# A projection by Strassen's seven products, interleaved with the first product, in a fused Mamba-2 and MoE kernel

## The chip, the cores and the metric

The kernel runs on one core of a Trainium2 chip. The metric is device time in microseconds (us) of one execution. Executions of one kernel mostly agree within 0.5% (four runs before: 420.35 to 421.12 us).

## The reference, cut to what matters

A chunked Mamba-2 scan over 4 batches, 8 heads and 768 steps gives 3072 tokens of 256 features, which go through a feed-forward block in fp32:

```python
def _moe_ref(x, w_in, w_out):          # x 3072x256, w_in 256x2048, w_out 2048x256
    h = x @ w_in
    g = h * (1.0 / (1.0 + np.exp(-1.702 * h)))
    return (g @ w_out).astype(np.float32)
```

`x @ w_in` is called the hidden product below, `g @ w_out` the projection. Both have the same number of multiplications.

## The kernel before

Tokens go in six groups of 512 (`NG` = 6). For a group the kernel does 16 hidden blocks of 128 features (`NF` = 16), each with a SiLU on ScalarE, then the projection. The scan of the next group (turn, gain, scores, finish) is placed among the hidden blocks. The kernel uses PSUM as eight banks of 128x512 fp32. Four go round as single banks (`bank`, tag "ff"). The other four are one area (`area`, tag "cb", one buffer), which holds the scores.

```python
    def bank(name):
        return ps.tile([P, 4 * P], FP32, tag="ff", name=name)          # pool: bufs=4

    def area(name):
        return ps.tile([P, R, 4 * P], FP32, tag="cb", name=name, bufs=1)
    ...
    def hidden(g, gT, f):
        h = bank(f"h{g}_{f}")
        for k in range(NK):
            nc.tensor.matmul(out=h, lhsT=w_in[:, k, f * P:(f + 1) * P], rhs=yT[g][:, k],
                             start=(k == 0), stop=(k == NK - 1))
        nc.scalar.activation(gT, h, AF.Silu, scale=GELU_SCALE)
    ...
    def project(g, gT, k):                     # 128 tokens; four of these in a group
        o = bank(f"o{g}_{k}")[:, :DM]
        for f in range(NF):
            nc.tensor.matmul(out=o, lhsT=gT[f][:, k * P:(k + 1) * P], rhs=w_out[:, f],
                             start=(f == 0), stop=(f == NF - 1))
        store(g, k, o)                         # VectorE scales it, SP stores 128 KB
```

Group 0 uses another order of the same matmuls (`project_all`), as the weights are still being unpacked from fp64; the change keeps that.

The kernel fixes the program's order on each engine (its `in_order`): what is emitted behind another instruction of the same engine stands behind it in that engine's queue and, in the timelines below, does not start before it.

## Time and profile before

| | before |
|---|---|
| time, median of 4 runs of the first comparison | 420.69 us (420.35 to 421.12) |
| span of the profiled execution | 418.8 us |
| TensorE busy | 401.9 us, 96% |
| VectorE busy | 163.6 us, 39% |
| group 3, hidden stage and projection | 63.1 us |
| end of the last projection to the end of the span | 3.2 us |

A busy share is an average over the span. The row of tenths tells where in the span it falls; from 90 us on TensorE is full. PEclk is the TensorE clock that was granted, in tenths of full speed; a "5" is half the clock, and an engine at half the clock still counts as busy. So the two rows have to be read together. The prediction shows these lines.

### The profile page before, as it was taken

The numbers are of one execution on the slowest core, as the hardware profiler recorded it, in microseconds if no ns is written. First come the engines' busy times: TensorE is split into PE (matmuls) and PEld (weight loads), VectorE is DVE, ScalarE is ACT, GpSimd is POOL, SyncE is SP. The second block draws the span as 40 slices with busy tenths as digits, with TensorE's granted clock in tenths as the row PEclk, the third lists the DMA queues.
The fourth block names the chain that finished last, engine by engine and source line by source line (L and its number), as shares of the span: only waits on it lengthen the run. The fifth ranks groups of instructions, "written<-read, shape, count | busy, mean of one in ns | idle before, by whom it ended". The sixth has DMA issues, their size and how long they took to land.

```text
span 418.8 us, 5032 instructions
## 1 busy us (share of the span) xinstructions
PE 401.9 (96%) x2046; PEld 257.9 (62%) x2046; DVE 163.6 (39%) x233; ACT 111.4 (27%) x212; POOL 8.9 (2%) x28
## 2 busy tenths in 40 slices
PE   6889995989999999999999999999999999999997
PEld 2354444768544688544688644588644588644885
DVE  3899889683682225324125323025423000000000
ACT  4119964350233200223200223200233300133000
POOL 4100000010000000000000000000000000000000
PEclk9559997999999999999999999999999999999999
DMA  8888929700492000591000590000000000000000
GB/s 188 162 184 199 351 94 131 222 0 2 87 202 101 2 13 25 73 232 49 1 14 25 70 211 35 0 13 27 13 2 0 2 13 25 14 0 0 13 14 26
DMA packets 86263, 29.66 MB, mean 71 GB/s; under 512 B 75936, under 2 KB 79200, under 8 KB 86240
## 3 DMA queue, kind: packets, MB, share of 16 engines
q1 hardware_dynamic: 84160, 29.07, 29.2%
q10 hardware_dynamic: 2080, 0.26, 0.4%
q8 instruction: 16, 0.26, 0.3%
q14 instruction: 7, 0.06, 0.0%
HBM read 26.08 MB, written 3.24 MB: 70 GB/s over the span
## 4 chain that ended last, share of the span: by engine, by line
PE 86%; DVE 5%; ACT 2%; DMA 2%; issue 2%; SPq 1%; POOL 0%; ACTq 0%; DVEq 0%; POOLq 0%
PE h L492 38%; PE o L506 33%; PE o L517 5%; PE area L402 3%; PE area L478 2%; DMA af<-in_a_dram 2%; PE area L470 1%; DVE L L267 1%; SPq L105 1%; PE area L428 1%; PE ab L284 1%; DMA az<-in_a_dram 1%; ACT CT L376 1%; PE cb L402 1%; DVE CsT L386 1%
## 5 line engine op out<-in xcount | busy, mean ns | idle before, releaser
L492 PE MATMUL h<-yT,w_in 128*128 128x512 f32 x384 | 173.9, 599 | 0.4 <-ACT yT L484 0.4
L506 PE MATMUL o<-w_out,gT 128*128 128x256 f32 x640 | 138.9, 379 | 0.0
L506 PEld LDWEIGHTS o<-w_out,gT 128*128 128x128 f32 x640 | 121.6, 190 | 18.7 <-issue 2.4
L492 PEld LDWEIGHTS h<-yT,w_in 128*128 128x128 f32 x384 | 70.2, 190 | 79.8 <-issue 76.7
L495 ACT ACTIVATE gT<-h 128x512 f32<-128x512 f32 x96 | 57.0, 595 | 223.4 <-PE h L492 223.4
L499 DVE TENSOR_SCALAR ob<-o 128x256 f32<-128x256 f32 x24 | 10.1, 424 | 170.6 <-PE o L506 161.9
L267 DVE TENSOR_TENSOR_SCAN L<-a,idents 128x1024 f32<-128x1024 f32 x18 | 41.1, 2281 | 0.0
L517 PE MATMUL o<-w_out,gT 128*128 128x256 f32 x128 | 32.3, 410 | 0.0
L412 DVE TENSOR_TENSOR L<-L,area 128x2048 f32<-128x2048 f32 x10 | 22.9, 2286 | 19.4 <-PE area L402 19.4
L517 PEld LDWEIGHTS o<-w_out,gT 128*128 128x128 f32 x128 | 25.7, 206 | 5.0 <-issue 1.2
L386 DVE TENSOR_TENSOR CsT<-area,since 128x256 f32<-128x256 f32 (+1 forms) x10 | 3.8, 383 | 42.6 <-ACT CT L376 42.6
L146 ACT ACTIVATE z<-e,edge 128x512 f32<-128x512 uint32 x16 | 11.4, 712 | 12.8 <-DVE e L142 12.8
L307 DVE TENSOR_TENSOR_SCAN L<-ab,idents 128x512 f32<-128x512 f32 x12 | 13.7, 1205 | 1.9 <-PE ab L284 1.9
L284 PE MATMUL ab<-X,ones 32*128 32x512 f32 x24 | 9.9, 804 | 2.6 <-DVE S L442 1.6
L147 ACT ACTIVATE p<-z,edge 128x512 uint32<-128x512 f32 x16 | 11.6, 723 | 0.5
L402 PEld LDWEIGHTS area<-CT,BT 32*128 32x128 f32 x160 | 7.2, 184 | 6.9 <-issue 6.4
L402 PE MATMUL area<-CT,BT 32*128 32x256 f32 x160 | 11.5, 400 | 0.0
L141 ACT ACTIVATE m<-bits 128x512 f32<-128x512 uint32 x16 | 10.7, 670 | 1.6 <-DVE w_out L170 1.6
L162 DVE SCALAR_TENSOR_TENSOR m<-u,m 128x512 f32<-128x512 f32 x16 | 11.0, 685 | 0.0
L164 DVE SCALAR_TENSOR_TENSOR p<-bits,p 128x512 uint32<-128x512 uint32 x16 | 11.0, 685 | 0.0
L478 PE MATMUL area<-L,x 128*32 128x128 f32 x320 | 10.8, 276 | 0.0
L484 ACT ACTIVATE yT<-area 128x256 f32<-128x256 f32 x20 | 6.6, 381 | 15.8 <-PE area L478 15.8
(68 smaller groups left out, 160.4 us busy)
## 6 DMA issues: line engine op xcount, KB each, us to landing
a<-scratch SPq DMA_DIRECT2D x18, 512.0 KB, 7.1
bits<-in_moe_w_in_dram SPq DMA_DIRECT2D x8, 512.0 KB, 5.2
bits<-in_moe_w_out_dram SPq DMA_DIRECT2D x8, 512.0 KB, 4.5
out_dram<-ob SPq DMA_DIRECT2D x24, 128.0 KB, 1.7
x<-in_x_dram SPq DMA_DIRECT2D x22, 128.0 KB, 2.9
b<-in_B_dram SPq DMA_DIRECT2D x24, 64.0 KB, 3.3
c<-in_C_dram SPq DMA_DIRECT2D x24, 64.0 KB, 2.7
af<-in_a_dram SPq DMA_DIRECT2D x4, 384.0 KB
```

What stands on the lines that cost most here:

```text
L146: nc.scalar.activation(z, e, AF.Relu, scale=-8.0, bias=edge[:, 0:1])
L147: nc.scalar.activation(p2, z, AF.Relu, scale=-1.0, bias=edge[:, 1:2])
L267: nc.vector.tensor_tensor_scan(out=Ls[p][:, k].rearrange("p r q i -> p (r q i)"), data0=ra.pop(n), data1=idents.rearrange("p h i -> p (h i ...
L284: nc.tensor.matmul(out=ab, lhsT=ones[rows], rhs=fans[p][rows].rearrange("p k q i -> p (k q i)"), start=True, stop=True, tile_position=(32 ...
L307: nc.vector.tensor_tensor_scan(out=flat[p][:, r], data0=ab, data1=idents.rearrange("p h i -> p (h i)")[:, :2 * Q * P], initial=0.0, op0=AL ...
L402: nc.tensor.matmul(out=cb[:, r, k], lhsT=BT[rows, k], rhs=CT[rows, k].rearrange("p q i -> p (q i)"), start=True, stop=True, tile_position= ...
L412: nc.vector.tensor_tensor(out=Lv, in0=Lv, in1=cb.rearrange("p r k e -> p k r e"), op=ALU.mult)
L478: nc.tensor.matmul(out=y[t][D * q:D * q + D, k], lhsT=rx[p][:, k, h], rhs=L[:, k, h // Q, h % Q], start=False, stop=True, tile_position=(0 ...
L492: nc.tensor.matmul(out=h, lhsT=w_in[:, k, f * P:(f + 1) * P], rhs=yT[g][:, k], start=(k == 0), stop=(k == NK - 1))
L495: nc.scalar.activation(gT, h, AF.Silu, scale=GELU_SCALE)
L506: nc.tensor.matmul(out=o, lhsT=gT[f][:, k * P:(k + 1) * P], rhs=w_out[:, f], start=(f == 0), stop=(f == NF - 1))
L517: nc.tensor.matmul(out=o[k // 2][:, k % 2], lhsT=gT[f][:, k * P:(k + 1) * P], rhs=w_out[:, f], start=(f == 0 and k % 2 == 0), stop=(f == N ...
```

## The change

The intent: each pair of feature blocks is treated as a 2x2 block product (two feature blocks, two halves of the outputs, two halves of the tokens). Strassen's scheme in Winograd's form needs seven block products where the direct way needs eight. The sums of weight blocks are made once (`mix_w`), those of activations per group (`mix_g`), all on VectorE. Seven accumulators of half a bank each lie in the four-bank area. The products of a group are interleaved with its hidden blocks (steps H and P). At the end of a group `combine` makes the four result blocks from the seven, and `give` transposes them back, as they come out with features on the partitions. The core of the diff:

```diff
+    def product(g, j):
+        if j == 0:
+            acc[g] = area(f"acc{g}").rearrange("p r (t e) -> p r t e", t=2)
+        B = gT.pop((g, j)).rearrange("p i (t e) -> p i t e", t=2)
+        T = mixed_g.pop((g, j))
+        A, S = w_out[:, 2 * j:2 * j + 2], mixed_w[j]
+        for r, t, lhsT, rhs in (
+                (0, 0, A[:, 0, :P], B[:, 0, 0]),
+                (0, 1, A[:, 1, :P], B[:, 1, 0]),
+                (1, 0, S[:, 1], T[:, 2]),
     ... four more of the seven
+            nc.tensor.matmul(out=acc[g][:, r, t], lhsT=lhsT, rhs=rhs, ...)
+
+    def combine(g):
+        a = acc.pop(g).rearrange("p r t e -> p (r t) e")
     ... tiles u and c
+        nc.scalar.activation(u[:, 0:4:3], a[:, 0:4:3], AF.Copy)
+        for o, v, w in ((u[:, 2], a[:, 2], u[:, 0]),
+                        (u[:, 1:3], a[:, 3:5], u[:, 2:3].to_broadcast([P, 2, HT])),
+                        (c[:, 0], a[:, 1:6:4], u[:, 0:2]),
+                        (c[:, 1, 1], u[:, 2], u[:, 3]),
+                        (c[:, 1, 0], a[:, 6], u[:, 2])):
+            nc.vector.tensor_tensor(out=o, in0=v, in1=w, op=ALU.add)
     ...
+            at(places, "H0", lambda g=g: combine(g - 1))
+            at(places, "H1", lambda g=g: mix_g(g, 0), lambda g=g: give(g - 1))
+            if g + 1 < NG:
+                at(places, "H0", lambda n=n: score(n), lambda n=n: weigh(n))
+                at(places, "H1", lambda n=n: score(n + 1), lambda n=n: weigh(n + 1))
     ...
+        for step in steps:                     # H0 H1 H2 P0 H3 P1 ... P4 H7 P5 P6 P7
+            j = int(step[1:])
+            if step[0] == "H":
+                hidden(g, 2 * j)
+                hidden(g, 2 * j + 1)
+            else:
+                product(g, j)
+            for do in after[g].get(step, []):
+                do()
     ...
+    combine(NG - 1)
+    give(NG - 1)
```

What is listed "at H0" is emitted after the two hidden blocks of step H0, so behind their SiLUs.

More of the change, by code (lines that the diff above doesn't have):

```diff
@@ L178, in spread @@
     def spread(n):
-        ra[n] = wide.tile([P, NH * P], FP32, tag="bits", name=f"a{n}", bufs=AHEAD + 2)
+        if n - 4 in ra:
+            ra[n] = ra[n - 4]
+        else:
+            ra[n] = wide.tile([P, NH * P], FP32, tag="bits", name=f"a{n}", bufs=AHEAD + 2)
         b, c = divmod(n, NC)
@@ L267, in decay @@
         nc.vector.tensor_tensor_scan(
-            out=Ls[p][:, k].rearrange("p r q i -> p (r q i)"), data0=ra.pop(n),
+            out=Ls[p][:, k].rearrange("p r q i -> p (r q i)"), data0=ra[n],
             data1=idents.rearrange("p h i -> p (h i)"), initial=0.0, op0=ALU.mult, op1=ALU.add)
@@ L353, in turn @@
         since_start(p)
+    shared = range(PG, 2 * PG)
     def bank(name):
@@ L362, in turn_only @@
         s = st[p] = {}
-        if p >= PG:
+        if p in shared:
             s["area"] = area(f"area{p}")
-        tp = s["area"][:, 0] if p >= PG else bank(f"tp{p}")
+        tp = s["area"][:, 0] if p in shared else bank(f"tp{p}")
         tp = tp.rearrange("p (j k i) -> p j k i", j=2, k=2)
@@ L396, in score @@
         BT, CT = s.pop("BT"), s.pop("CT")
-        cb = s["area"] if p >= PG else area(f"cb{p}")
+        cb = s["area"] if p in shared else area(f"cb{p}")
         cb = cb.rearrange("p r (k e) -> p r k e", k=2)
@@ L422, in gain @@
         nk = 1 if c + 2 == NC else 2
-        A = st[p]["area"][:, 1] if p >= PG else bank(f"A{p}")
+        A = st[p]["area"][:, 1] if p in shared else bank(f"A{p}")
         A = A[:, :2 * Q * D].rearrange("p (k e) -> p k e", k=2)
@@ L460, in finish @@
             yT[g] = ffn.tile([P, NK, TG], FP32, tag="yT", name=f"yT{g}")
-        y = [s["area"][:, t] if p >= PG else bank(f"y{p}_{t}") for t in range(NK)]
+        y = [s["area"][:, t] if p in shared else bank(f"y{p}_{t}") for t in range(NK)]
         y = [v[:, :2 * P].rearrange("p (k i) -> p k i", k=2) for v in y]
@@ L486, in finish, with hidden @@
                 y[t].rearrange("p k i -> p (k i)"), AF.Copy)
-    def hidden(g, gT, f):
+    gT = {}
+    HT = TG // 2
+    def hidden(g, f):
+        j, i = divmod(f, 2)
+        if i == 0:
+            gT[g, j] = ffn.tile([P, 2, TG], FP32, tag="gT", name=f"gT{g}_{j}", bufs=NF // 2)
         h = bank(f"h{g}_{f}")
@@ L493, in hidden, with store, out_tile, project_all @@
                              start=(k == 0), stop=(k == NK - 1))
-        nc.scalar.activation(gT, h, AF.Silu, scale=GELU_SCALE)
-    def store(g, k, o):
-        ob = ffn.tile([P, DM], FP32, tag="ob", name=f"ob{g}_{k}", bufs=2)
-        nc.vector.tensor_single_scalar(out=ob, in_=o, scalar=1.0 / GELU_SCALE, op=ALU.mult)
-        r0 = g * TG + k * P
-        nc.sync.dma_start(out=out[r0:r0 + P, :], in_=ob)
-    def project(g, gT, k):
-        o = bank(f"o{g}_{k}")[:, :DM]
-        for f in range(NF):
-            nc.tensor.matmul(out=o, lhsT=gT[f][:, k * P:(k + 1) * P], rhs=w_out[:, f],
-                             start=(f == 0), stop=(f == NF - 1))
-        store(g, k, o)
-    def project_all(g, gT, between):
+        nc.scalar.activation(gT[g, j][:, i], h, AF.Silu, scale=GELU_SCALE)
+    def store(g, half, ob):
+        r0 = g * TG + half * HT
+        nc.sync.dma_start(out=out[r0:r0 + HT, :].rearrange("(k p) d -> p k d", p=P), in_=ob)
+    def out_tile(g, half):
+        return ffn.tile([P, 2, DM], FP32, tag="ob", name=f"ob{g}_{half}", bufs=2)
+    def project_all(g, between):
         o = [bank(f"o{g}_{j}").rearrange("p (k e) -> p k e", k=2) for j in range(CG // 2)]
@@ L516, in project_all @@
             for k in range(CG):
-                nc.tensor.matmul(out=o[k // 2][:, k % 2], lhsT=gT[f][:, k * P:(k + 1) * P],
+                nc.tensor.matmul(out=o[k // 2][:, k % 2],
+                                 lhsT=gT[g, f // 2][:, f % 2, k * P:(k + 1) * P],
                                  rhs=w_out[:, f], start=(f == 0 and k % 2 == 0),
                                  stop=(f == NF - 1), skip_group_check=True)
-        for k in range(CG):
-            store(g, k, o[k // 2][:, k % 2])
+        for half in range(2):
+            ob = out_tile(g, half)
+            nc.vector.tensor_single_scalar(out=ob, in_=o[half], scalar=1.0 / GELU_SCALE,
+                                           op=ALU.mult)
+            store(g, half, ob)
@@ new lines, with mix_w @@
+    mixed_w, mixed_g, acc, done = {}, {}, {}, {}
+    def mix_w(n):
+        t = wide.tile([P, 2, 4, P], FP32, tag="bits", name=f"mw{n}", bufs=AHEAD + 2)
+        w = w_out[:, 4 * n:4 * n + 4].rearrange("p (j i) (c e) -> p j i c e", i=2, c=2)
+        a11, a12, a21, a22 = w[:, :, 0, 0], w[:, :, 1, 0], w[:, :, 0, 1], w[:, :, 1, 1]
+        s1, s2, s3, s4 = (t[:, :, i] for i in range(4))
+        for o, u, v, op in ((s1, a21, a22, ALU.add), (s2, s1, a11, ALU.subtract),
+                            (s3, a11, a21, ALU.subtract), (s4, a12, s2, ALU.subtract)):
+            nc.vector.tensor_tensor(out=o, in0=u, in1=v, op=op)
+        for k in range(2):
+            mixed_w[2 * n + k] = t[:, k]
@@ new lines, in mix_g @@
+    def mix_g(g, j):
+        B = gT[g, j].rearrange("p i (t e) -> p i t e", t=2)
+        t = mixed_g[g, j] = ffn.tile([P, 4, HT], FP32, tag="gT", name=f"mg{g}_{j}", bufs=NF // 2)
+        nc.vector.tensor_tensor(out=t[:, 0:2], in0=B[:, :, 1], in1=B[:, 0], op=ALU.subtract)
+        nc.vector.tensor_tensor(out=t[:, 2], in0=B[:, 1, 1], in1=t[:, 0], op=ALU.subtract)
+        nc.vector.tensor_tensor(out=t[:, 3], in0=B[:, 1, 0], in1=t[:, 2], op=ALU.subtract)
+    def product(g, j):
[8 more added lines that the diff above has]
+                (1, 0, S[:, 1], T[:, 2]),
+                (1, 1, S[:, 0], T[:, 0]),
+                (2, 0, S[:, 2], T[:, 1]),
+                (2, 1, S[:, 3], B[:, 1, 1]),
+                (3, 0, A[:, 1, P:], T[:, 3])):
+            nc.tensor.matmul(out=acc[g][:, r, t], lhsT=lhsT, rhs=rhs,
+                             start=(j == 0 and t == 0), stop=(j == NF // 2 - 1),
+                             skip_group_check=True)
@@ new lines, in combine @@
+    def combine(g):
+        a = acc.pop(g).rearrange("p r t e -> p (r t) e")
+        u = ffn.tile([P, 4, HT], FP32, tag="gT", name=f"u{g}", bufs=NF // 2)
+        c = done[g] = ffn.tile([P, 2, 2, HT], FP32, tag="gT", name=f"c{g}", bufs=NF // 2)
+        nc.scalar.activation(u[:, 0:4:3], a[:, 0:4:3], AF.Copy)
[5 more added lines that the diff above has]
+            nc.vector.tensor_tensor(out=o, in0=v, in1=w, op=ALU.add)
@@ new lines, in give @@
+    def give(g):
+        c = done.pop(g)
+        for t in range(2):
+            o = bank(f"oT{g}_{t}").rearrange("p (k e) -> p k e", k=2)
+            for k in range(2):
+                for i in range(2):
+                    nc.tensor.transpose(out=o[:, k, i * P:(i + 1) * P],
+                                        in_=c[:, i, t, k * P:(k + 1) * P], identity=ident)
+            ob = out_tile(g, t)
+            nc.scalar.activation(ob, o, AF.Copy, scale=1.0 / GELU_SCALE)
+            store(g, t, ob)
@@ L592 @@
         at(in_project[0], i, lambda k=k: spread(2 * CG + k))
-    for k, i in enumerate((0, 1, 5, 7)):
-        at(in_hidden[1], i, lambda k=k: decay(2 * CG + k))
-    scan_at(in_hidden[1], 2 * PG, (3, 4, 5, 8))
-    scan_at(in_hidden[1], 2 * PG + 1, (9, 10, 11, 14))
-    for g in range(1, NG - 1):
-        for j in range(PG if g > 1 else 0):
-            scan_at(in_hidden[g], (g + 1) * PG + j, [8 * j + i for i in (0, 1, 2, 6)])
-        if g + 2 < NG:
-            for k in range(CG):
-                at(in_project[g], k, lambda g=g, k=k: decay((g + 2) * CG + k))
@@ L605, with late @@
-    bring = {g: ((g + 2) * CG, (g + 3) * CG) for g in range(NG - 2)}
-    for g in range(NG):
+    after = [{} for _ in range(NG)]
+    for g in range(1, NG):
+        n, places = (g + 1) * PG, after[g]
+        chunks = range((g + 2) * CG, (g + 3) * CG) if g + 2 < NG else ()
+        if g == 1:
+            def late(p):
+                gain(p)
+                keep(p)
+                score(p)
+                weigh(p)
+            at(places, "H0", lambda: decay(2 * CG), lambda: decay(2 * CG + 1), lambda: turn(n1))
+            n1 = n
+            at(places, "H1", lambda: late(n1), lambda: decay(2 * CG + 2),
+               lambda: decay(2 * CG + 3), lambda: turn(n1 + 1))
+            at(places, "H3", lambda: finish(n1), lambda: late(n1 + 1))
+            at(places, "H4", lambda: finish(n1 + 1))
+            for k, i in enumerate(("H4", "P0", "P2", "P4")):
+                at(places, i, lambda k=k: mix_w(k))
+            for j in range(NF // 2):
+                at(places, f"P{j - 1}" if j else "H4", lambda j=j: mix_g(1, j))
+        else:
+            at(places, "H0", lambda g=g: combine(g - 1))
[3 more added lines that the diff above has]
+                at(places, "H1", lambda n=n: score(n + 1), lambda n=n: weigh(n + 1))
+            at(places, "H2", lambda g=g: mix_g(g, 1))
+            for j in range(2, NF // 2):
+                at(places, f"P{j - 2}", lambda g=g, j=j: mix_g(g, j))
+            if g + 1 < NG:
+                at(places, "H2", lambda n=n: finish(n))
+                at(places, "P0", lambda n=n: finish(n + 1))
+        for k, c in enumerate(chunks):
+            at(places, f"P{k + 1}", lambda c=c: decay(c))
+        if g + 2 < NG:
+            for k in range(PG):
+                p = (g + 2) * PG + k
+                at(places, f"P{5 + k}", lambda p=p: turn(p), lambda p=p: gain(p),
+                   lambda p=p: keep(p))
@@ L607 @@
+    for f in range(NF):
+        hidden(0, f)
+        for do in in_hidden[0].get(f, []):
+            do()
+    project_all(0, in_project[0])
+    for g in range(1, NG):
         if g + 2 < NG:
-            for j in range(PG if g else 0):
-                load((g + 2) * PG + j)
+            for k in range(PG):
+                load((g + 2) * PG + k)
             for b in range(NB):
@@ L612 @@
                     spread_rows(b)
-        gT = []
-        for f in range(NF):
-            gT.append(ffn.tile([P, TG], FP32, tag=f"gT{f}", name=f"gT{g}_{f}", bufs=1))
-            hidden(g, gT[f], f)
-            for do in in_hidden[g].get(f, []):
-                do()
-        if 0 < g < NG - 2:
-            for n in range(*bring[g]):
-                spread(n)
-        if g == 0:
-            project_all(g, gT, in_project[g])
-            continue
-        for b in list(raf):
-            clip_rows(b)
-            decay_rows(b)
-        for k in range(CG):
-            project(g, gT, k)
-            for do in in_project[g].get(k, []):
-                do()
+                    at(after[g], "P4", lambda b=b: clip_rows(b), lambda b=b: decay_rows(b))
+        ahead = 5 if g == 1 else 3
+        steps = [f"H{j}" for j in range(ahead)]
+        for j in range(NF // 2):
+            steps += [f"P{j}"] + ([f"H{j + ahead}"] if j + ahead < NF // 2 else [])
+        for step in steps:
[3 more added lines that the diff above has]
+                hidden(g, 2 * j + 1)
+            else:
+                product(g, j)
+            for do in after[g].get(step, []):
+                do()
+            if g + 2 < NG and step in ("H1", "H3"):
+                for k in range(2):
+                    spread((g + 2) * CG + k + (2 if step == "H3" else 0))
+    combine(NG - 1)
+    give(NG - 1)
     in_order(tc)
```

## The prediction

It uses these figures of the kernel before. Behind the wait of 4.36 us, which ends when VectorE is done with the rotated C in the area that the gain products share with it, the trace has half the clock from 68.4 to 75.2 us, 6.8 us. An fp32 tensor_tensor of VectorE takes 423 ns for 256 columns, 692 for 512 and 2286 for 2048 (the rows of L386, L170 and L412).

> **What bounds the kernel now.** I read the page first, then the busy time by stage, then TensorE's timeline. The page's busy shares and slices:
>
> ```profile
> PE 401.9 (96%) x2046; PEld 257.9 (62%) x2046; DVE 163.6 (39%) x233; ACT 111.4 (27%) x212; POOL 8.9 (2%) x28
> PE   6889995989999999999999999999999999999997
> PEclk9559997999999999999999999999999999999999
> ```
>
> TensorE is full from about 90 us to the end; no other engine is half busy. Clock dips (5, 5, then 7) stand only in the first fifth. Busy time by stage, a projection and the hidden stage after it (columns: span, then PE, PEld, DVE, ACT, POOL, clock, DMA share, GB/s):
>
> ```profile
> 206.20:233.80 27.60, 27.60 (x129) 24.30 (x128) 8.74 (x9) 0.60 (x1) 0.00 (x0) 1.00 0.04 15
> 233.80:269.30 35.50, 35.45 (x205) 16.79 (x205) 9.69 (x12) 12.28 (x25) 0.00 (x0) 1.00 0.45 93
> ```
>
> Both are TensorE alone. There are six groups of 512 tokens; a middle one takes 206.22 to 269.35 = 63.1 us. Every microsecond of TensorE work taken out counts, and so does every one in which it stands still. TensorE's timeline gives the prices:
>
> ```profile
> 172.32 0.38 PE L369 MATMUL area<-ident,b 128*128 128x128 f32 x2
> 172.54 0.38 PE L369 MATMUL area<-ident,c 128*128 128x128 f32 x2
> ...
> 206.22 27.79 PE L506 MATMUL o<-w_out,gT 128*128 128x256 f32 x128
> ...
> 360.46 27.63 PE L492 MATMUL h<-yT,w_in 128*128 128x512 f32 x64
> ```
>
> The projection of a group is 16 x 4 = 64 matmuls of 256 columns, recorded as 128 passes: 27.63 us to the next stage, 0.216 us a pass, 0.432 us a matmul. One hidden block (two matmuls of 512, four passes of 0.429) is 1.72 us. Four transposes of 128x128 (one pass each) take 172.32 to 172.76 = 0.44 us, 0.11 us each.
>
> Why idleness can cost twice is shown where this kernel waits longest:
>
> ```profile
> 63.01 1.89 PE L517 MATMUL o<-w_out,gT 128*128 128x256 f32 x8
> 69.26 0.44 PE L428 MATMUL area<-x,Be 128*32 128x64 f32 x8 [4.36 <-DVE CsT L386]
> 69.63 8.20 PE L517 MATMUL o<-w_out,gT 128*128 128x256 f32 x24
> ```
> ```profile
> 66.00:68.00 2.00, 0.00 (x0) 0.00 (x0) 1.97 (x3) 0.31 (x1) 0.00 (x0) 1.00 1.12 119
> 68.00:70.00 2.00, 0.74 (x9) 0.57 (x10) 1.40 (x4) 0.00 (x0) 0.00 (x0) 0.60 1.04 143
> 70.00:72.00 2.00, 2.00 (x6) 1.56 (x6) 1.97 (x6) 1.09 (x2) 0.00 (x0) 0.50 1.01 102
> ```
>
> After 4.36 us of idleness the clock falls to 0.50, and the next 24 passes take 0.34 us each instead of 0.216: 3 us more. The same stage's wait of 1.76 us, before 90.07, leaves the clock at 1.00.
>
> [...]
>
> ```profile
> L386 DVE TENSOR_TENSOR CsT<-area,since 128x256 f32<-128x256 f32 x7 | 3.0, 423 | 30.4 <-ACT CT L376 30.4
> L170 DVE TENSOR_TENSOR w_out<-m,p 128x512 f32<-128x512 f32 x8 | 5.5, 692 | 0.3
> L412 DVE TENSOR_TENSOR L<-L,area 128x2048 f32<-128x2048 f32 x10 | 22.9, 2286 | 19.4 <-PE area L402 19.4
> ```
>
> **The change, part by part.** Groups 1 to 5 change; group 0 keeps its direct projection.
>
> *Removed.* 7 products of 256 columns instead of 8 for each of 8 pairs of blocks: 8 matmuls less a group, 8 x 0.432 = 3.45 us; five groups: -17.3 us, all on TensorE.
>
> *Added on TensorE.* The result comes out transposed: 8 transposes a group, 0.88 us. Four groups: +3.5 us; those of group 5 are in the tail below.
>
> *Added beside it.* VectorE gets sums of activations, three instructions for each pair: 0.69 + 0.42 + 0.42 = 1.53 us, 12.3 us a group; once, sums of weights, 16 x 0.42 = 6.8 us; a group's combination, five instructions. With scans (four of 2.28 us) and weighting (two of 2.29) that is some 33 us of VectorE in 63: it fits. In the interleaved part one product step (14 passes, 3.0 us) plus one hidden step (two blocks, 3.4 us) lasts 6.4 us, and the worst VectorE step (1.53 sums, 2.57 scan and its end, in two groups 2.3 for the decay rows) is run off before the step that needs it, as sums are made two steps ahead. I followed which instruction each wait in the built program names and found no other standstill there. Group 1, with sums one step ahead but five hidden steps first, waits perhaps 0.8 us for VectorE's scans. Buffers of sums and activations come free one step early.
>
> *The new wait.* The accumulators occupy the four-bank area that the scores also need. In the built order of groups 2, 3 and 4, TensorE does the first two hidden blocks and then the scores of the next group, which wait for the last of the combination's reads. The combination starts with a ScalarE copy that stands behind the SiLUs of those two blocks. When such blocks follow a projection in the kernel before (they begin at 360.46):
>
> ```profile
> 362.43 0.60 ACT L495 ACTIVATE gT<-h 128x512 f32<-128x512 f32 x1 [28.75 <-PE h L492]
> ...
> 364.15 0.60 ACT L495 ACTIVATE gT<-h 128x512 f32<-128x512 f32 x1 [1.12 <-PE h L492]
> ```
>
> The second SiLU starts 3.69 us after the blocks begin. The copy (128x512, about 0.6) then ends at 4.8. VectorE's five: 0.42 + 0.69 + 0.69, then two of 0.42 that overlap a little, with hand-overs: 2.6, so 7.4 us. TensorE has issued its blocks by 3.43. It stands 3.9 us, three times: **+11.8 us**. Group 5 has no scores, but its transposes after the second hidden step (6.9) wait until 7.4: +0.4.
>
> *The clock.* TensorE idles 3.8 us, and the 1.1 us of scores after it use 32 rows a matmul. [...] With a chance of a bit under a half for each of three: +3 to +3.5 expected, 0 to 9 possible (odds that I chose, as no trace shows a gap of this length). [...]
>
> *The tail.* Now the last projection is followed by:
>
> ```profile
> 415.75 0.42 DVE L499 TENSOR_SCALAR ob<-o 128x256 f32<-128x256 f32 x1 [6.48 <-PE o L506]
> ```
>
> and one store; from 415.56 to 418.8 it is 3.2 us. After the change, behind the last product: 0.2 to completion, copy 0.6, VectorE 2.6, transposes 0.6, two output copies from 4.05 to 5.1, and the store of 256 KB, 2.6 as now and some 0.4 more. That is 8.2: +5.0 us.
>
> Sum: -17.3 + 3.5 + 0.8 + 11.8 + 0.4 + 5.0 = +4.2, or 424.8 us at full clock; with some 2.3 of that loss (I shade it, as it may not come at all), 427.
>
> **The rivals.** (a) *The TensorE work decides*: if the wait for the area were short, 420.6 - 17.3 + 3.5 + 5 = 412. For it: TensorE is the bound, and 8 of 64 matmuls go. Against: the order of instructions is fixed, the copy cannot pass the SiLUs, and nothing of TensorE's can pass the scores. (b) *The clock falls at every boundary*: 424.8 + 9 = 434. For it: 4.36 us did it in this trace. Against: 1.76 us did not, 3.8 lies between[...]. (c) *VectorE becomes the bound of the interleaved part*: each of 40 steps late by 0.5 us gives 445. Against: 33 of 63 us, and sums two steps ahead.
>
> **Range and chances.** Without clock loss 424.8, give or take 1.5; with it up to 434. Range 422.5 to 433. Faster by over 2% is below 412.2: only rival (a), 0.04. Slower by over 2% is above 429.0: clock lost at two boundaries or more, 0.35. Within 2%: 0.61.
>
> **What would show it.** TensorE's idle time before the scores of groups 2 to 4: 3.8 us each, put down to VectorE's combination; if it is under 1 us, the main step is wrong. The clock in the stretch after them: 1.00 or 0.50. Product passes at 0.216 us and 112 a group; if 0.25 or more, the interleaving costs. Idle time before products after the first: near zero; if VectorE's sums are named there, rival (c). Last product to end: about 8 us. Group period 64.7 us against 63.1. I am wrong if the scores don't wait, or if the clock falls in stretches other than after those waits.

## More of the kernel before

Faster or slower means a difference of over 2%.

## The result, and the profile after

The changed kernel takes 430.58 us (median of 4 runs, 429.2 to 431.3) against 420.69. The ratio is 1.0231, with a 95% interval of 1.0202 to 1.026: slower. Ratios in this document are the mean time of one kernel's fast runs over that of the other's fast runs of the same rounds, so they are not quite the ratio of the medians quoted.

The page's shares and slices of the kernel after:

```profile
PE 395.3 (92%) x2006; PEld 251.5 (59%) x2006; DVE 232.5 (54%) x372; ACT 119.9 (28%) x227; POOL 8.9 (2%) x28
PE   6789995989999999699999699999699999999993
PEclk9559996999999999899999899999889999999997
```

TensorE is busy for 6.6 us less, so work was taken away, although part of that busy time now runs at half the clock. Yet the span grew by 8.7 us. There are three new notches in the row of tenths, each a "6", at equal distances, and a lower clock just behind each. They lie at the starts of groups 2, 3 and 4. TensorE's timeline at the first of them:

```profile
168.43 3.60 PE L508 MATMUL h<-yT,w_in 128*128 128x512 f32 x8
175.86 1.15 PE L412 MATMUL cb<-CT,BT 32*128 32x256 f32 x16 [3.84 <-DVE c L592]
176.94 5.40 PE L508 MATMUL h<-yT,w_in 128*128 128x512 f32 x8
```

The number in brackets is the idle time ahead of a row and what ended it. The scores (L412) stand 3.84 us and are released by VectorE's last sum of the combination (L592). The eight hidden passes behind them take 5.40 us, where eight behind scores at full clock take 3.70. ScalarE and VectorE in the same stretch show what the time goes into:

```profile
170.39 0.60 ACT L511 ACTIVATE gT<-h 128x512 f32<-128x512 f32 x1 [4.17 <-issue]
172.06 0.60 ACT L511 ACTIVATE gT<-h 128x512 f32<-128x512 f32 x1 [1.07 <-PE h L508]
172.55 0.59 ACT L586 ACTIVATE u<-acc 128x512 f32<-128x512 f32 x1
```
```profile
173.18 1.15 DVE L592 TENSOR_TENSOR u<-acc,u 128x256 f32<-128x256 f32 x2 [5.46 <-ACT u L586]
174.36 0.69 DVE L592 TENSOR_TENSOR c<-acc,u 128x512 f32<-128x512 f32 x1
174.97 0.41 DVE L592 TENSOR_TENSOR c<-u 128x256 f32<-128x256 f32 x1
175.30 0.42 DVE L592 TENSOR_TENSOR c<-acc,u 128x256 f32<-128x256 f32 x1
```

The accumulators are complete at about 168.6, but the copy of the combination (L586) starts at 172.55, as two SiLUs stand ahead of it in the queue, and the second of them needs hidden blocks that end at 172. Then VectorE's chain runs to 175.72. In all groups together, from the view of waits (us in total, times, longest):

```profile
PE cb L412 <- DVE c L592: 11.5, 3, 3.8
```

The clock in the first wait and behind it, in stretches of 2 us (the first figure behind the comma is TensorE's busy time, the clock is the figure ahead of the last two):

```profile
172.00:174.00 2.00, 0.02 (x1) 0.00 (x0) 0.79 (x2) 1.08 (x2) 0.00 (x0) 1.00 0.00 0
174.00:176.00 2.00, 0.14 (x4) 0.17 (x8) 1.68 (x4) 0.00 (x0) 0.00 (x0) 1.00 0.00 0
176.00:178.00 2.00, 2.00 (x18) 1.24 (x19) 0.93 (x1) 0.00 (x0) 0.00 (x0) 0.85 0.00 0
178.00:180.00 2.00, 2.00 (x3) 0.67 (x2) 1.97 (x3) 0.00 (x0) 0.00 (x0) 0.50 0.00 0
180.00:182.00 2.00, 2.00 (x5) 0.86 (x4) 0.84 (x2) 0.60 (x1) 0.00 (x0) 0.79 0.00 0
```

The clock stays at 1.00 while TensorE stands, and is then lower by half for (1 - 0.85 + 1 - 0.50 + 1 - 0.79) x 2 / 0.5 = 3.4 us. After the second wait it is 3.4 us again, after the third 6.8 us. Comparing the rows behind each wait (scores, then eight hidden passes) with 1.15 and 3.70 at full clock gives the loss: 5.40 - 3.70 = 1.70; 1.78 + 4.72 - 4.85 = 1.65; 2.09 + 5.70 - 4.85 = 2.94. Together 6.3 us.

The products themselves, from the groups, and the tail, from the timeline of all engines:

```profile
L575 PE MATMUL acc<-mg,mw 128*128 128x256 f32 x240 | 58.3, 379 | 0.0
```
```profile
418.57 0.59 PE L575 MATMUL acc<-mg,w_out 128*128 128x256 f32 x2
419.26 0.60 ACT L586 ACTIVATE u<-acc 128x512 f32<-128x512 f32 x1 [8.53 <-PE acc L575]
...
422.48 1.14 PE L600 MATMUL oT<-ident,c 128*128 128x128 f32 x7 [0.34 <-DVE c L592]
423.07 1.19 ACT L603 ACTIVATE ob<-oT 128x512 f32<-128x512 f32 x2 [3.21 <-PE oT L600]
423.69 0.97 SPq L515 DMA_DIRECT2D out_dram<-ob  x2
```

The products on sums have no idle time ahead of them (the last figure, 0.0). The last pass is issued by 419.0 (418.57 and two of 0.216), and the span ends at 427.5: 8.5 us in place of 3.2.

An account of the two spans: products -17.3 (five groups, 8 matmuls of 0.432 us less), transposes of four groups +3.5, three waits of 4.0 us of lost issue (171.86 to 175.86) +12.0, clock +6.3, tail +5.3, a wait of 0.2 at group 5's transposes. The sum is +10.0, the spans differ by 8.7. The 1.3 us left over were not pursued; turn and gain now follow each other directly, which may save hand-overs, but that is not shown.

### The profile page after: what moved, and what is told of

Read it like the earlier page. It is cut to its first block, busy times and chain, and to the rows that moved or that the text cites. A ratio compares the mean times of both kernels' runs of the same rounds, so it can differ in the third digit from the quotient of the medians.

```text
span 427.5 us, 5052 instructions
## 1 busy us (share of the span) xinstructions
PE 395.3 (92%) x2006; PEld 251.5 (59%) x2006; DVE 232.5 (54%) x372; ACT 119.9 (28%) x227; POOL 8.9 (2%) x28
## 4 chain that ended last, share of the span: by engine, by line
PE 84%; DVE 8%; issue 2%; DMA 2%; ACT 2%; SPq 1%; DVEq 0%; POOL 0%; ACTq 0%; POOLq 0%
PE h L508 39%; PE acc L575 29%; PE o L527 5%; PE cb L412 3%; PE y L488 2%; DVE c L592 2%; PE y L480 1%; DMA af<-in_a_dram 1%; DVE u L592 1%; SPq L110 1%; PE oT L600 1%; DVE L L275 1%; PE tp L379 1%; PE ab L292 1%; ACT u L586 1%
## 5 line engine op out<-in xcount | busy, mean ns | idle before, releaser
L557 DVE TENSOR_TENSOR mg<-gT 128x512 f32<-128x512 f32 x40 | 27.5, 688 | 91.5 <-ACT gT L511 88.4
L575 PE MATMUL acc<-mg,mw 128*128 128x256 f32 x240 | 58.3, 379 | 0.0
L575 PEld LDWEIGHTS acc<-mg,mw 128*128 128x128 f32 x240 | 45.6, 190 | 6.2
L575 PE MATMUL acc<-gT,w_out 128*128 128x256 f32 x160 | 42.1, 386 | 0.0
L575 PEld LDWEIGHTS acc<-gT,w_out 128*128 128x128 f32 x160 | 29.6, 190 | 15.2 <-issue 11.5
L527 PE MATMUL o<-w_out,gT 128*128 128x256 f32 x128 | 32.3, 410 | 0.0
L527 PEld LDWEIGHTS o<-w_out,gT 128*128 128x128 f32 x128 | 25.6, 206 | 5.0 <-issue 1.2
L412 PE MATMUL cb<-CT,BT 32*128 32x256 f32 x160 | 17.0, 495 | 11.5 <-DVE c L592 11.5
L592 DVE TENSOR_TENSOR u<-acc,u 128x256 f32<-128x256 f32 (+1 forms) x10 | 5.6, 558 | 36.3 <-ACT u L586 36.1
L575 PE MATMUL acc<-gT,mw 128*128 128x256 f32 x80 | 23.8, 379 | 0.0
L575 PE MATMUL acc<-mg,w_out 128*128 128x256 f32 x80 | 23.8, 379 | 0.0
L412 PEld LDWEIGHTS cb<-CT,BT 32*128 32x128 f32 x160 | 10.9, 231 | 16.3 <-issue 14.7
L559 DVE TENSOR_TENSOR mg<-gT,mg 128x256 f32<-128x256 f32 x40 | 17.0, 425 | 1.4
L558 DVE TENSOR_TENSOR mg<-gT,mg 128x256 f32<-128x256 f32 x40 | 17.0, 424 | 1.4
```

The lines of the kernel that those rows point to most:

```text
L412: nc.tensor.matmul(out=cb[:, r, k], lhsT=BT[rows, k], rhs=CT[rows, k].rearrange("p q i -> p (q i)"), start=True, stop=True, tile_position= ...
L527: nc.tensor.matmul(out=o[k // 2][:, k % 2], lhsT=gT[g, f // 2][:, f % 2, k * P:(k + 1) * P], rhs=w_out[:, f], start=(f == 0 and k % 2 == 0 ...
L557: nc.vector.tensor_tensor(out=t[:, 0:2], in0=B[:, :, 1], in1=B[:, 0], op=ALU.subtract)
L558: nc.vector.tensor_tensor(out=t[:, 2], in0=B[:, 1, 1], in1=t[:, 0], op=ALU.subtract)
L559: nc.vector.tensor_tensor(out=t[:, 3], in0=B[:, 1, 0], in1=t[:, 2], op=ALU.subtract)
L575: nc.tensor.matmul(out=acc[g][:, r, t], lhsT=lhsT, rhs=rhs, start=(j == 0 and t == 0), stop=(j == NF // 2 - 1), skip_group_check=True)
```

## The experiments

The theory: the time is lost in one wait, of the scores for the accumulators, which is long only because the combination is queued behind two SiLUs, and in the half clock that this idleness brings. Rivals: VectorE's new sums, or the switching between two kinds of matmul, slow the interleaved part; or the clock falls for a reason other than idleness. Each run had three rounds beside the kernel before on the same chip (before: 420.86 in the first four, 420.59 in the last four, single runs 420.16 to 423.2). All results were correct. The argument rests on how the runs differ from the changed kernel and from each other.

### The combination first

```diff
-            at(places, "H0", lambda g=g: combine(g - 1))
...
+        if g > 1:
+            combine(g - 1)
         for step in steps:
```

> Only change: the combination of a group (its ScalarE copy and five VectorE sums) is put ahead of the first two hidden blocks of the next group, not behind their SiLUs. Theory (the scores' wait for the accumulators, and the half clock after it, cost the time): the copy starts 0.2 us after the last product, the sums end 3.3 us later, so the scores are free at 3.5 us against 3.43; three waits of 3.84 us go to under 0.4 us each, the clock stays at 1.00 after group 0, and the time is 412 to 414 us. Rival A (VectorE's sums or the mix of matmuls in the interleaved part cost the time): stays above 425. Rival B (the waits matter but the clock loss has another cause): about 419.

Measured: 411.86 us (410.8 to 414.0), ratio 0.9794 (0.9762 to 0.9825). It does the same work as the changed kernel, with 3 x 6 instructions of the group boundaries moved ahead of two hidden blocks (and 6 at group 5), and takes 18.7 us less. Its timeline at the first boundary, all engines:

```profile
170.43 3.60 PE L508 MATMUL h<-yT,w_in 128*128 128x512 f32 x8
170.69 0.60 ACT L586 ACTIVATE u<-acc 128x512 f32<-128x512 f32 x1 [2.46 <-PE acc L575]
...
173.45 0.42 DVE L592 TENSOR_TENSOR c<-acc,u 128x256 f32<-128x256 f32 x1
...
174.01 1.15 PE L412 MATMUL cb<-CT,BT 32*128 32x256 f32 x16
175.09 3.70 PE L508 MATMUL h<-yT,w_in 128*128 128x512 f32 x8
```

The copy starts 0.26 us after the first hidden pass, not 4.1. The scores have no bracket: TensorE waits for nothing, and the passes behind them take 3.70 us. The expectation was met but for 0.1 us (412 to 414 was expected), and rivals A and B fall: sums and interleaving are all still there, and the clock loss went with the wait (the clock is 1.00 from 170.43 us to 402.7).

### The scores one step later

```diff
-                at(places, "H0", lambda n=n: score(n), lambda n=n: weigh(n))
-                at(places, "H1", lambda n=n: score(n + 1), lambda n=n: weigh(n + 1))
+                at(places, "H1", lambda n=n: score(n), lambda n=n: weigh(n))
+                at(places, "H2", lambda n=n: score(n + 1), lambda n=n: weigh(n + 1))
```

> The combination stays behind the SiLUs; the scores of the next group's two pairs are moved one hidden step later each. Theory: the wait shrinks from 3.84 us to about 0.5 us at the transposes and up to 0.7 us at the first product, the clock stays at 1.00, 415 to 418 us. Rival (it is the combination's own length or its place that costs, whoever comes after it): no change from 430.

Measured: 416.38 us (414.64 to 417.14), ratio 0.9889 (0.9861 to 0.9917). The combination is as late as in the changed kernel, but its consumer comes later. What is left are waits of 0.21 us at the transposes and up to 0.97 at the first product, which needs the area that the second scores now leave later:

```profile
184.99 1.13 PE L575 MATMUL acc<-gT,w_out 128*128 128x256 f32 x4 [0.97 <-DVE L L422]
```

So it is the distance between the combination and its consumer that counts, not where the combination stands.

### Filling the wait, whole and half

```diff
+                at(places, "H0", lambda: fill(4))      # in the second run fill(2)
+    def fill(n):
+        t = bank("fill")
+        for i in range(n):
+            nc.tensor.matmul(out=t, lhsT=ones, rhs=ones.unsqueeze(1).to_broadcast([P, 4, P]),
+                             start=True, stop=True, skip_group_check=True)
```

(The line stands between the combination and the scores, for groups 2 to 4.)

> As the changed kernel, but TensorE does four matmuls of 512 columns on constants (8 passes, 3.43 us) into a spare bank just ahead of the waiting scores; nothing reads them. The wait for the combination is not shortened; TensorE is merely busy in it. Theory: idle time falls under 0.6 us each, the clock stays at 1.00, and the time falls by the clock loss alone (about 6.3 us): 424 to 425. Rival (the half clock comes from something else than the idleness): 430 or more, clock as now.

Measured: 423.78 us (423.51 to 424.03), ratio 1.0071 (1.0056 to 1.0086). Unread matmuls made the kernel 6.8 us faster than the changed one. The waits are 1.2 us in total, and the clock is 1.00 from 160 us to 380. This prices the two halves of the loss apart: 6.8 us for the clock, and from here to the run with the combination first another 11.9 us for the wait.

> The same with two matmuls (4 passes, 1.72 us), which leaves about 2.1 us idle before the scores. [...] no fall, 424 to 425. [...] some or all of the three falls remain, 426 to 431. The wait of 1.76 us in the kernel before did not do it.

Measured: 423.88 us median, but 423.68 to 426.8; ratio 1.0096 (1.0057 to 1.0134). In the profiled run a wait was

```profile
176.66 1.15 PE L419 MATMUL cb<-CT,BT 32*128 32x256 f32 x16 [2.12 <-DVE c L599]
```

and the clock stayed at 1.00 from 160 to 380 us. Of the two outcomes, no fall or some of the three, the profiled run has the first, with a wait of 2.12 us; the changed kernel lost the clock behind waits of 3.84. The one run at 426.8 had a mean clock of 0.949, against 0.958 to 0.962 in the other three. It has no trace of its own, so where it lost the clock is not shown.

### The interleaving without Strassen

```diff
+    def product(g, j):
+        if j == 0:
+            acc[g] = area(f"acc{g}")
+        B = gT.pop((g, j))
+        for i in range(2):
+            for k in range(CG):
+                nc.tensor.matmul(out=acc[g][:, k // 2, (k % 2) * DM:(k % 2 + 1) * DM],
+                                 lhsT=B[:, i, k * P:(k + 1) * P], rhs=w_out[:, 2 * j + i], ...)
     ... combine: two scaled copies by VectorE and two stores, ahead of H0; no sums, no transposes
```

> The interleaving of hidden and product steps and the early combination are kept, but each product step does the eight direct matmuls (no sums, no combination, no transposes; two banks of the area copied out by VectorE, 2 x 0.69 us, before the scores need it). Theory (interleaving is free, Strassen's seven of eight products is what gains): as the kernel before within 1.5 us, 420 to 422 us, so that the seven products with their transposes back are worth 8 to 10 us net against the run with the combination first. Rival (switching between the two kinds of matmul costs): over 424.

Measured: 421.11 us (420.27 to 422.89), ratio 1.0005 (0.9964 to 1.0045). Interleaving alone neither costs nor gains. The seven products are therefore worth 421.11 - 411.86 = 9.3 us net, tail and transposes included. (The two runs came on different chips; by their ratios to the kernel before, 1.0005 - 0.9794, it is 8.9 us.)

### The sums twice

```diff
         nc.vector.tensor_tensor(out=t[:, 0:2], in0=B[:, :, 1], in1=B[:, 0], op=ALU.subtract)
+        nc.vector.tensor_tensor(out=t[:, 0:2], in0=B[:, :, 1], in1=B[:, 0], op=ALU.subtract)
```

(On top of the combination first.)

> As the run with the combination first, but the first of the three sums of each block pair is done twice: VectorE gets 0.69 us more in each of 40 steps, 5.5 us a group. Theory (VectorE has slack behind TensorE): 411.5 to 414, within 2 us of that run. Rival (VectorE is near the bound of the interleaved part): 417 or more, up to 439 if every step is late.

Measured: 412.67 us (412.4 to 413.67), ratio 0.9803 (0.9764 to 0.9843). VectorE works 27 us more (260.2 us busy against 233 in the run without the doubling), and the time moves by 0.8 us. One wait appears, in group 1, where sums are made one step ahead:

```profile
164.06 1.56 PE L576 MATMUL acc<-mg,mw 128*128 128x256 f32 x6 [0.99 <-DVE mg L559]
```

So VectorE is not the bound, and group 1 is the place where it is nearest.

### The last group direct

```diff
-    combine(NG - 1)
-    give(NG - 1)
+    for k in range(CG):
+        g = NG - 1
     ... as project() of the kernel before, from the new tiles
```

(On top of the combination first; group 5 has its hidden blocks first, then this.)

> As the run with the combination first, but group 5, behind which nothing hides the combination and the transposes, keeps the direct projection with its hidden stage ahead of it. It gives back 3.45 us of products and gets the old tail of 3.2 us for one of 9.0. Theory: 411.9 - 9.0 + 3.2 + 3.45 = about 409.5 us. Rival (the tail is set by the store alone): 413 or more.

Measured: 410.25 us (409.54 to 411.11), ratio 0.9742 (0.9709 to 0.9776). The gain is 1.6 us where 2.4 was expected; the two runs came in different rounds, and both of them spread by more than 1.5 us, so the size is uncertain.

### Filling the waits of group 0

```diff
+    at(in_project[0], 1, lambda: fill(5))
+    at(in_project[0], 8, lambda: fill(2))
```

(On top of the last group direct. The kernel before has these waits too.)

> As the run with the last group direct, and TensorE does unread matmuls on constants in the two waits of group 0's projection (4.3 us in the wait of 4.36, 1.7 us in that of 1.76), which the kernel before has too. Theory (idleness alone halves the clock): no half clock after 35 us, 3 us less for the first and 0 to 1.7 for the second, which halved the clock in only some runs: 405 to 407 us, and a smaller spread between runs. Rival: no change from the run with the last group direct.

Measured: 407.41 us (406.66 to 408.18), ratio 0.9674 (0.9641 to 0.9707): the fastest, 13.2 us under the kernel before, and 0.4 us over what the theory allowed. The clock row of its page:

```profile
PEclk9558999999999999999999999999999999999999
```

There is no half clock left after the start. Compared with the run before it this is 2.8 us. The trace of that run has some 3.4 us of half clock behind each of the two waits of group 0 (mean clock 0.91 from 60 to 80 us, 0.94 from 80 to 107), so about 1.7 us were lost at each.

The wait of 1.76 us in group 0 adds something. In the kernel before, and then in the run with the combination first, the same place of the same work reads:

```profile
90.07 0.43 PE L428 MATMUL area<-x,Be 128*32 128x64 f32 x16 [1.76 <-DVE CsT L386]
90.43 3.72 PE L517 MATMUL o<-w_out,gT 128*128 128x256 f32 x16
```
```profile
90.17 0.43 PE L438 MATMUL area<-x,Be 128*32 128x64 f32 x16 [1.76 <-DVE CsT L396]
90.53 5.41 PE L527 MATMUL o<-w_out,gT 128*128 128x256 f32 x16
```

The same idle time costs nothing in one execution and 1.7 us in another. Behind this wait the clock was read in seven traces: it is 0.50 from 92 to 95 us with the combination first and with the direct products interleaved, 0.50 from 91 to 94 with the last group direct, and stays at 1.00 in four (before, after, scores later, sums twice).

## Why the prediction was right or wrong

By its range (422.5 to 433.0) the prediction held at 430.58. The point, 427.0, was 3.6 us low, and the largest single chance, 0.61, was put on within 2%; it came 2.3% slower.

- **The wait**: 3.9 us, three times, named with its cause, from the built order and the durations before. The trace has 4.0 us of lost issue, 3.84 of idleness, and the run with the combination first shows that nothing else made it long. Right.
- **The gain of the products**: the 14 passes of one step took 3.02 us in the trace (154.35 to 157.37), 0.216 each as assumed, with no idle time ahead of them. The run that keeps the direct products confirms the net worth, 9.3 us; the prediction's own terms give 17.3 - 3.5 - 5.0 = 8.8. Right.
- **The clock** is the term that was mis-sized. The prediction counted 2.3 us, shaded down from 3 to 3.5, from "a chance of a bit under a half for each of three", odds that were the author's estimate, as no trace then had a gap of this length. Measured: 6.3 us in the trace, 6.8 by filling the wait; the clock fell at all three.

  What stood ahead of the falls: the changed kernel's trace has them at 177.42, 242.27 and 307.12 us, 64.85 us from one to the next. All falls in the clock records of this trace and of that of the kernel before lie whole multiples of 3.41 us apart, and the half clock lasted 3.41, 3.41 and 6.83 us. So stretches of 3.41 us are compared here. In the one ahead of the second fall TensorE idled for 3.0 us, ahead of the third for 3.1. The one ahead of the first (174.0 to 177.4) holds 1.86 us of idleness, 1.1 us of scores of 32 rows and 0.5 us of hidden passes. The one before that (170.6 to 174.0) holds 1.98 us of idleness and 1.4 us of hidden passes, and the clock was still 1.00 from 174.0 to 177.4. So the idle time of such a stretch did not by itself tell whether the clock fell. What decides is not shown by these runs, nor what odds would have been right. The mean clocks point to falls in the runs without a trace too: (1 - mean clock) x span / 0.5 gives 45 to 52 us of half clock in each of the four runs of the changed kernel, 32 to 35 in those with the whole wait filled. With 6.3 in place of 2.3 the sum would have been 431, partly by luck, as the 0.8 us of the next point did not come.
- **Group 1's wait for VectorE**, 0.8 us: none; the trace shows that stage full. **Group 5's transposes**, 0.4: 0.2. **The tail**, +5.0: +5.3. Small. **The period of a group** was put at 64.7 us, though its own terms give 63.1 - 3.45 + 0.88 + 3.9 = 64.4; the trace has 66.0, in which the half clock is 1.7 to 2.9.
- **Rivals**: (a) was ruled out by the order of the queues as stated, and what it would have needed (412) is what the run with the combination first reached, 411.86. (b) is what happened, for two thirds of its 9 us. (c) fell: doubling a sum cost 0.8 us.

## What to carry to other kernels

When an accumulator's memory is shared with the next user, look at what stands ahead of its first reader in that reader's own queue: two activations that depend on later matmuls made no wait at all into one of 4 us. When a busy TensorE loses a few microseconds, count the clock as well: 3.84 us of idleness cost another 1.7 to 2.9 us each time here, and 1.76 us another 1.7 us in some executions; cover what cannot be removed with unread matmuls (they gained 6.8 us in one kernel here and 2.8 us in another). Price a saving of matmuls together with its end: the last group has nothing to hide the combination behind, and may be better off without it.
